# Attention and two feed-forward layers on one core: the four differences of g in the second layer's first product move from VectorE to GpSimd

## The chip, the core and the metric

The kernel runs on one core of one Trainium2 chip. A core has a TensorE (PE in the profile; its weight loads are a row of their own, PEld), a VectorE (DVE), a ScalarE (ACT), a GpSimd (POOL) and a SyncE (SP), which here issues the DMA transfers. Each engine executes its own list of instructions in order, and the engines wait for each other by semaphores. The metric is the device time of the program in microseconds (us); lower is better. The granted TensorE clock is the upper of the two levels (2.4 GHz, shown as 1.00) in all windows below.

## The reference

```python
attn_out = _attn_ref(q, k, v)          # causal attention, window of 64, 4 x 8 heads, 576 x 64
x = attn_out.transpose(0, 2, 1, 3).reshape(2304, 512)
...
r = np.maximum(x @ w_in1, 0.0)         # layer one
x = (r * r) @ w_out1
...
h = x @ w_in2                          # layer two: (2304, 512) @ (512, 2048)
g = np.maximum(0.01 * h, h)
return g @ w_out2                      # (2304, 2048) @ (2048, 512)
```

All arrays are float32. The change lies in the third part, layer two.

## The kernel before

Attention and layer one fill the time up to about 490 us and are not touched. Layer two has two stages, both with a 2 x 2 block scheme of seven products in place of eight: the blocks are called 11, 12, 21 and 22, their sums s1 to s4 on the one side and t1 to t4 on the other. Every product is made with operands that are split in a high and a low part (hi by a cast on ACT, lo = value - hi by a subtraction on DVE, the helpers at L346 and L349) and takes three matmuls: hi hi, hi lo, lo hi.

**First product** (`pair`, L889 to L985). A pair is a choice of one of three pieces of 768 tokens (s) and one of eight pairs of 128 columns of h (p); there are 24. The first six run over p = 0 and 1, then p = 2 to 7 come each with the three pieces. A pair has seven products of six 128x384 matmuls (L889), which collect in four PSUM banks: h, acc, s and t. ACT copies a bank into another as its start (a seed) or into a tile named e, DVE adds (L913) into the pair's tile of g (named m, four blocks of 384), and ACT applies the leaky function (L920) to each block. Then `combine` (L968 to L976) makes four differences for the second stage, in three instructions: the two of tile ta in one (128x768: g1 - g0 and g2 - g1), and the two of tile tb one after the other (128x384: g2 less the first of ta, and g3 less that result). `keep` (L925 to L930) sends g0, the pair g2 and g3, ta and tb to DRAM, as four transfers named gd<-m (twice), gd<-g and gd<-wst. tb lies in the pool "wst" of three tiles, which is also that of the weights wf before they are split; in the last two pairs tb lies in pool "g", which holds ta.

Two things share the engines with the pairs. `x_combos` (L770 to L810) loads a piece of x into a tile m (L773), makes differences in place (L797) and splits them. `w_in` (L841 to L861) loads two blocks of weights into a wst tile (L821, wst<-wf), makes their sums (L835) and splits both. Each is due when the first pair that uses its operands comes near.

**Second product** (`superblock`, L1039 to L1136). For each of the three pieces of tokens seven products of 48 matmuls (L1071) follow. `fetch` (L1025) loads what `keep` stored (w<-gd, m<-gd), `operands` splits it in four units of 128x768, and `w_out` (L995) loads the weights' blocks in two halves (L1001, wst<-wq, 128x1024) and splits those. A product's matmuls go unit by unit, and the tile of a unit is used again by a later product. The first of these products run between the last three pairs.

The order on each engine is not written by hand. Each step is given to a planner with an engine, a cost, a due time, the tiles that it reads and those that it writes; the planner plays the program through with these costs and so gets the order in which the instructions are written for all engines, in which turn the tiles of a pool are given out, and in which order SP issues its transfers. Only the order is kept: on the chip an instruction starts when its engine is free and its semaphores have come. For a step of n elements per partition on DVE the planner reckons `0.15 + n * 0.00106`.

Of the kernel before, what the change touches and what calls it, by code (L numbers as in the profile page):

```python
# [14 lines left out]
ALU = mybir.AluOpType  # L15
# [22 lines left out]
NH = 384  # L38
# [58 lines left out]
class Plan:  # L97
# [38 lines left out]
    def slot(self, pool, tag, shape, dtype=F32, bufs=1):  # L136
        self.bufs.setdefault(tag, bufs)
        return Slot(self, pool, tag, shape, dtype)

    def op(self, engine, cost, due, fn, reads=(), writes=(), needs=(), nbytes=0, margin=0.0, after=()):  # L140

        i = len(self.ops)
        deps = set(after)
        for r in reads:
            if r in self.last_write:
                deps.add(self.last_write[r])
            self.reads_since[r].append(i)
        for w in writes:
            if w in self.last_write:
                deps.add(self.last_write[w])  # L150
            deps.update(self.reads_since.pop(w, ()))
            self.last_write[w] = i
        deps.discard(i)
        slots = {x[0] for x in (*reads, *writes) if isinstance(x[0], Slot)} | set(needs)
        for s in slots:
            s.users += 1
        self.ops.append((engine, cost, due, fn, deps, slots, nbytes, margin))
# [103 lines left out]

def dve_cost(n):
    return 0.15 + n * 0.00106


def dve_fast(n):
# [29 lines left out]
def build(ctx, tc, qp, kp, vp, w1, w2, caps, ident, out, prm=PRM):  # L296
    nc = tc.nc
# [22 lines left out]
    class Late:  # L320

        pool = None
# [12 lines left out]
    op, slot = plan.op, plan.slot  # L335
# [29 lines left out]
    def float_words(s, j, m, c, cv, after=()):  # L365
# [34 lines left out]
        op("act", act_cost(DM), c - prm["AL"], rebias, [(raw, 0)], [(raw, 0)])  # L400
        op("dve", dve_fast(DM), c, conv0, [(raw, 0)], [(cv, 0)])
        op("dve", dve_cost(DM), c + 0.4 * cs, conv1, [(raw, 0)], [(cv, 0)])
        op("dve", dve_cost(DM), c + 1.0 * cs, conv2, [(raw, 0)], [(cv, 0)])

    def weight(k, c, gate=()):

        j, m = divmod(k, 2)
        cv = slot(ep, "e", [P, DM], I32, 4)
        w = slot(rings[f"w{m}"], f"w{m}", [P, 2, DM], F32R)
        wt[j, m] = w  # L410
        cs = prm["CS"]
        float_words(0, j, m, c, cv)
        op("act", act_cost(DM), c + 1.8 * cs, lambda: copy(w.ap[:, 0], f32(cv.ap)), [(cv, 0), *gate], [(w, 0)])
        op(
            "dve", dve_cost(DM), c + 2.5 * cs,
            lambda: sub(nc.vector, w.ap[:, 1], f32(cv.ap), w.ap[:, 0]),
            [(cv, 0), (w, 0)], [(w, 1)],
        )
# [455 lines left out]
    def pair(q, s, p, T, A, last):  # L874
# [93 lines left out]
        def combine(own, k, n, in0, in1, due):  # L968
            views = [(lambda o=o, j=j: o.ap[:, j : j + n]) for o, j in (in0, in1)]
            op(  # L970
                "dve", dve_cost(n * NH), due,
                lambda: nc.vector.tensor_tensor(out=own.ap[:, k : k + n], in0=views[0](), in1=views[1](), op=ALU.subtract),
                [(o, j + h) for o, j in (in0, in1) for h in range(n)], [(own, k + h) for h in range(n)],
            )

        combine(ta, 0, 2, (g, 1), (g, 0), t[8])  # L976
        combine(tb, 0, 1, (g, 2), (ta, 0), t[9])
        combine(tb, 1, 1, (g, 3), (tb, 0), t[9] + 0.6)
        keep(1, lambda: g.ap[:, 2:4], [(g, 2), (g, 3)], t[9])
        keep(3, lambda: ta.ap, [(ta, 0), (ta, 1)], t[9])  # L980
# [210 lines left out]
    if prm["WARM"]:  # L1191
# [3 lines left out]
        for i in range(prm["WARM"]):  # L1195
# [3 lines left out]
                    out=warm_p.ap, lhsT=warm_s.ap, rhs=warm_s.ap, start=True, stop=True  # L1199
# [76 lines left out]
    for q, (p, s) in enumerate(seq):  # L1276
# [4 lines left out]
        if q == len(seq) - 2:  # L1281
            unit_slots()
            plan.pad = 8192
            own = [[slot(rings[t], t, [P, HP, NH]) for t in ("w0", "w1")] for _ in range(2)]
# [68 lines left out]
```

## Time and profile before

| what | value |
|---|---|
| three timed executions, us | 840.36, 841.39, 841.53 |
| their median, us | 841.39 |
| the profiled execution, us | 840.72 |
| its span from the first instruction to the last, us | 838.9 |
| busy share of the span: PE, PEld, DVE, ACT, POOL | 99%, 90%, 67%, 55%, 0% |
| granted TensorE clock | 1.0 |

The span is what the trace covers; 1.8 us of the profiled execution lie outside it. A busy share is the time in which the engine had an instruction in execution, over the whole span. PE's matmuls are pipelined, so that its rows overlap a little and a gap of PE is best read from the row of PEld, which shows when a weight load had to wait and for whom.

### The profile page before, as it was taken

Reading aid. Unit: us, or ns where it says so; the run is one execution under the profiler, and the core shown is the slowest. Engines: PE = TensorE matmul, PEld = TensorE weight load, DVE = VectorE, ACT = ScalarE, POOL = GpSimd, SP = SyncE. Lnnn points to the kernel's source line nnn. Section 1 sums busy time; section 2 is a strip of 40 time slices with the busy share of each in tenths; the row PEclk is TensorE's granted clock in tenths of the full one; section 3 lists DMA queues with packets and bytes.
Section 4 is the critical chain, followed back from the end, with each engine's and each line's share of the span. In section 5 each row is a group of like instructions: output and inputs, shape, how many; then the busy total and the mean of one; then the engine's idle time right before and its main releaser. Section 6 shows DMA issues by size and latency. Waiting matters only on the chain.

```text
span 838.9 us, 14060 instructions
## 1 busy us (share of the span) xinstructions
PE 830.2 (99%) x5344; PEld 751.0 (90%) x5344; DVE 562.7 (67%) x941; ACT 463.7 (55%) x1011; POOL 0.2 (0%) x4
## 2 busy tenths in 40 slices
PE   9999999999999999999999999999999999999998
PEld 8788988888888888888888899999999999999998
DVE  5988687865656666567899657665654887555553
ACT  4978865644354554354444456655565877444441
POOL 0000000000000000000000000000000000000000
PEclk9999999999999999999999999999999999999999
DMA  8665434225434355346874256665557998766661
GB/s 288 220 211 188 146 111 147 83 80 200 144 128 146 129 198 169 127 151 201 298 244 151 73 185 238 223 222 207 209 207 256 373 416 329 247 207 227 206 207 57
DMA packets 77988, 164.64 MB, mean 196 GB/s; under 512 B 6752, under 2 KB 46432, under 8 KB 77920
## 3 DMA queue, kind: packets, MB, share of 16 engines
q1 hardware_dynamic: 77472, 163.21, 56.9%
q8 instruction: 42, 0.69, 0.3%
q10 hardware_dynamic: 448, 0.52, 0.3%
q14 instruction: 26, 0.21, 0.1%
HBM read 108.66 MB, written 55.05 MB: 195 GB/s over the span
## 4 chain that ended last, share of the span: by engine, by line
PE 89%; DMA 5%; DVE 4%; ACT 1%; issue 0%; SPq 0%; ACTq 0%; DVEq 0%
PE h L686 22%; PE acc L698 21%; PE acc L1071 10%; PE h L889 8%; PE s L889 5%; PE h L1071 5%; PE h L698 3%; PE acc L889 3%; PE s L1071 2%; PE t L889 2%; PE t L1071 2%; PE t L552 2%; PE s L479 1%; DMA gd<-g 1%; PE t L543 1%; DMA w<-vp 1%
## 5 line engine op out<-in xcount | busy, mean ns | idle before, releaser
L686 PE MATMUL h<-x,w 128*128 128x512 f32 (+1 forms) x1008 | 214.7, 364 | 1.5 <-DVE x L349 1.3
L686 PEld LDWEIGHTS h<-x,w 128*128 128x128 f32 x1008 | 168.3, 188 | 32.3 <-issue 1.7
L698 PE MATMUL acc<-g,w 128*128 128x512 f32 x576 | 141.5, 392 | 0.0
L698 PEld LDWEIGHTS acc<-g,w 128*128 128x128 f32 x576 | 107.2, 188 | 21.9
L889 PE MATMUL h<-w,x 128*128 128x384 f32 x432 | 83.0, 334 | 0.0
L889 PEld LDWEIGHTS h<-w,x 128*128 128x128 f32 x432 | 75.6, 188 | 0.1
L1071 PE MATMUL acc<-x,w 128*128 128x384 f32 x360 | 73.8, 334 | 0.1
L349 DVE TENSOR_TENSOR x<-m,x 128x768 fp32r<-128x768 f32 x50 | 47.2, 957 | 36.3 <-ACT x L346 36.2
L346 ACT CAST x<-m 128x768 fp32r<-128x768 f32 x50 | 41.2, 837 | 40.9 <-PE h L1071 17.4
L1071 PEld LDWEIGHTS acc<-x,w 128*128 128x128 f32 x360 | 63.4, 188 | 0.4 <-DVE w L349 0.4
L379 ACT ACTIVATE wst<-wst 128x512 f32<-128x512 f32 x64 | 42.7, 673 | 34.0 <-DMA wst<-w1b 14.5
L346 ACT CAST w<-m 128x768 fp32r<-128x768 f32 (+1 forms) x50 | 39.5, 798 | 39.3 <-PE h L1071 10.8
L349 DVE TENSOR_TENSOR w<-m,w 128x768 fp32r<-128x768 f32 (+1 forms) x50 | 44.9, 907 | 20.5 <-ACT w L346 20.3
L657 DVE TENSOR_TENSOR e<-e 128x512 f32<-128x512 f32 x48 | 33.1, 690 | 37.9 <-ACT g L656 37.8
L889 PE MATMUL s<-w,x 128*128 128x384 f32 x288 | 57.8, 335 | 0.0
L652 ACT ACTIVATE e<-h 128x512 f32<-128x512 f32 x48 | 28.5, 594 | 47.2 <-PE h L686 46.1
L889 PEld LDWEIGHTS s<-w,x 128*128 128x128 f32 x288 | 50.5, 188 | 0.4 <-ACT e L346 0.3
L698 PE MATMUL acc<-x,w 128*128 128x512 f32 x192 | 48.1, 394 | 0.0
L388 DVE SCALAR_TENSOR_TENSOR e<-wst,e 128x512 int32<-128x512 int32 x64 | 44.3, 692 | 1.9
L394 DVE SCALAR_TENSOR_TENSOR e<-wst,e 128x512 int32<-128x512 int32 x64 | 44.1, 690 | 1.5
L698 PEld LDWEIGHTS acc<-x,w 128*128 128x128 f32 x192 | 34.6, 189 | 6.3
L511 ACT ACTIVATE u<-u,nm 128x128 f32<-128x128 f32 x64 | 25.0, 392 | 25.4 <-DVE nm L508 25.4
(131 smaller groups left out, 1319.5 us busy)
## 6 DMA issues: line engine op xcount, KB each, us to landing
m<-gd SPq DMA_DIRECT2D x38, 768.0 KB, 4.4
wst<-wq SPq DMA_DIRECT2D x22, 512.0 KB, 7.6
gd<-g SPq DMA_DIRECT2D x26, 384.0 KB, 3.1
gd<-m SPq DMA_DIRECT2D x24, 384.0 KB, 2.7
gd<-wst SPq DMA_DIRECT2D x22, 384.0 KB, 3.2
wst<-w1a SPq DMA_DIRECT2D x16, 512.0 KB, 4.4
v<-vp SPq DMA_DIRECT2D x32, 256.0 KB, 3.3
wst<-w2a SPq DMA_DIRECT2D x16, 512.0 KB, 3.6
```

What stands on the lines that cost most here:

```text
L346: nc.scalar.copy(out=dst, in_=src)
L349: eng.tensor_tensor(out=lo, in0=src, in1=f32(hi), op=ALU.subtract)
L379: nc.scalar.activation(out=top, in_=top, func=AF.Copy, scale=2.0**-112)
L388: nc.vector.scalar_tensor_tensor(out=cv.ap, in0=words(1), scalar=-(1 << 31), in1=cv.ap, op0=ALU.bitwise_and, op1=ALU.bitwise_or,)
L394: nc.vector.scalar_tensor_tensor(out=cv.ap, in0=words(0), scalar=29, in1=cv.ap, op0=ALU.logical_shift_right, op1=ALU.bitwise_or,)
L511: nc.scalar.activation(out=u.ap[:, h, :], in_=u.ap[:, h, :], func=AF.Exp, bias=nm.ap[:, h : h + 1], scale=1.0, accum_out=None if dve_sum e ...
L652: nc.scalar.activation(out=r.ap, in_=hp.ap, func=AF.Relu)
L657: op("dve", dve_cost(n), a0 + 1.4, lambda: nc.vector.tensor_tensor(out=r.ap, in0=r.ap, in1=r.ap, op=ALU.mult), [], [(r, 0)])
L686: nc.tensor.matmul(out=hp.ap, lhsT=wi[:, a, kk, :], rhs=x.ap[:, b, kk, c0 : c0 + n], start=(kk == 0 and m == 0), stop=(kk == KD - 1 and m ...
L698: nc.tensor.matmul(out=a, lhsT=w.ap[:, i, d * P : (d + 1) * P], rhs=g[:, b], start=first and m == 0, stop=last and m == 2, skip_group_chec ...
L889: nc.tensor.matmul(out=ps.ap, lhsT=wc.ap[:, v, k, i * P : (i + 1) * P], rhs=x.ap[:, u, n], start=begin and i == 0 and m == 0, stop=i == 1 ...
L1071: nc.tensor.matmul(out=bank[into][i].ap, lhsT=w.ap[:, v, p, i * P : (i + 1) * P], rhs=u.ap[:, x, e, j], start=begin and n == 0 and j == 0 ...
```

## The change

The three instructions of `combine` in each pair are given to GpSimd, as `nc.gpsimd.tensor_tensor`, and the planner reckons them with a cost of their own. Nothing else of the program text changes. Of the changed kernel all lines behind L266 have numbers that are higher by four.

```diff
@@ -263,6 +263,10 @@
+def pool_cost(n):
+    return 0.2 + n * 0.0021
+
+
 def dve_fast(n):
     return 0.15 + n * 0.00053
...
@@ -968,8 +972,8 @@
         def combine(own, k, n, in0, in1, due):
             views = [(lambda o=o, j=j: o.ap[:, j : j + n]) for o, j in (in0, in1)]
             op(
-                "dve", dve_cost(n * NH), due,
-                lambda: nc.vector.tensor_tensor(out=own.ap[:, k : k + n], in0=views[0](), in1=views[1](), op=ALU.subtract),
+                "pool", pool_cost(n * NH), due,
+                lambda: nc.gpsimd.tensor_tensor(out=own.ap[:, k : k + n], in0=views[0](), in1=views[1](), op=ALU.subtract),
                 [(o, j + h) for o, j in (in0, in1) for h in range(n)], [(own, k + h) for h in range(n)],
             )
```

72 instructions leave DVE's list, 24 of 128x768 and 48 of 128x384, and stand on GpSimd's, which held nothing in the main part of the program. With the other engine and cost the planner comes to another order on all engines. Three places of it matter below.

The first is SP's list while the first pairs run. gd<- are `keep`'s transfers (wst is tb, g is ta, m is g itself), and m<-x_103 are the three loads of a piece of x. Before:

```order
L928 DMA gd<-m 128x2x384
L928 DMA gd<-g 128x2x384
L928 DMA gd<-wst 128x2x384
L773 DMA m<-x_103 128x768
L773 DMA m<-x_103 128x384 x2
```

After:

```order
L932 DMA gd<-m 128x2x384
L932 DMA gd<-g 128x2x384
L777 DMA m<-x_103 128x768
L932 DMA gd<-wst 128x2x384
L777 DMA m<-x_103 128x384 x2
```

The first load of x now stands ahead of the store of tb, the other two behind it as before.

The second is SP's list in the middle of the pairs, about a `w_in`, whose two loads are wst<-wf. The rows run from one pair's last stores to the stores of the next. Before:

```order
L928 DMA gd<-m 128x384
L928 DMA gd<-g 128x2x384
L928 DMA gd<-m 128x2x384
L928 DMA gd<-wst 128x2x384
L821 DMA wst<-wf 128x512 x2
L928 DMA gd<-g 128x2x384
```

After:

```order
L932 DMA gd<-wst 128x2x384
L932 DMA gd<-m 128x384
L825 DMA wst<-wf 128x512 x2
L932 DMA gd<-m 128x2x384
L932 DMA gd<-g 128x2x384
L932 DMA gd<-wst 128x2x384
```

Before, the loads follow the store of tb of a pair; after, the store of g0 of the next pair (gd<-m 128x384) stands between that and the loads.

The third is ACT's list where the pairs give way to the second product. The casts of 128x768 are units of operands fetched from gd, w_6559<-wst is the first half of the weights s1 of the second of these products, and w_6484<-m, after it was renumbered w_6465<-m, is the first unit of an operand used later, whose tile was the third unit's of the first of these products. Before:

```order
L346 CAST x_6518<-w_6321 128x768 x2
L920 ACTIVATE m<-m 128x384 x2
L346 CAST x_6404<-w_6342 128x768 x2
L346 CAST w_6559<-wst 128x1024
L346 COPY e<-acc_306 128x384
L346 COPY e<-acc_276 128x384
L346 CAST w_6484<-m 128x768
```

After:

```order
L350 CAST x_6519<-w_6319 128x768
L924 ACTIVATE m<-m 128x384
L350 CAST x_6519<-w_6319 128x768
L350 CAST w_6465<-m 128x768
L350 CAST w_6559<-wst 128x1024
L350 COPY e<-acc_306 128x384
L350 COPY e<-acc_276 128x384
```

The cast of w<-m has moved from behind the two copies to ahead of the cast of the weights.

## Rows read from the trace of the kernel before

**Rows 1.** Page, part 1: busy us by engine, share of the span, instructions.
```profile
PE 830.2 (99%) x5344; PEld 751.0 (90%) x5344; DVE 562.7 (67%) x941; ACT 463.7 (55%) x1011; POOL 0.2 (0%) x4
```

**Rows 2.** Windows: busy us by engine (and instructions), granted clock, DMA share, GB/s.
```profile
core 0: us, PE busy (x) PEld busy (x) DVE busy (x) ACT busy (x) POOL busy (x), PEclk, DMA share, GB/s
...
497.00:508.00 11.00, 10.66 (x60) 10.03 (x59) 10.83 (x17) 8.21 (x16) 0.00 (x0) 1.00 0.83 286
...
562.00:584.00 22.00, 22.00 (x129) 22.00 (x128) 13.05 (x23) 12.84 (x28) 0.00 (x0) 1.00 0.61 212
...
650.00:676.00 26.00, 25.75 (x147) 25.11 (x146) 21.47 (x27) 19.81 (x32) 0.00 (x0) 1.00 1.03 379
...
760.00:838.90 78.90, 75.50 (x436) 75.18 (x434) 37.12 (x46) 30.34 (x41) 0.00 (x0) 1.00 0.52 174
```

**Rows 3.** Waits of PEld from 470 to 690: us in total, times, longest.
```profile
PEld acc L889 <- ACT acc L346: 1.5, 2, 0.9
PEld t L889 <- ACT m L920: 0.5, 1, 0.5
PEld acc L1071 <- DVE w L349: 0.4, 1, 0.4
PEld s L889 <- ACT e L346: 0.3, 1, 0.3
```

**Rows 4.** Instructions of L972: ns min/median/max, first and last start, form.
```profile
L972 DVE TENSOR_TENSOR g<-m x24: 949/959/960, 497.3 to 665.8; 128x768 f32<-128x768 f32 x24
L972 DVE TENSOR_TENSOR wst<-m,g x22: 557/559/560, 498.3 to 648.1; 128x384 f32<-128x384 f32 x22
```

**Rows 5.** Timeline, first pairs: start, us, engine, line, operation [idle before <-releaser].
```profile
491.27 1.01 PEld L889 LDWEIGHTS acc<-w,x 128*128 128x128 f32 x6 [0.87 <-ACT acc L346]
...
499.97 1.52 SPq L773 DMA_DIRECT2D m<-x  x3
...
502.78 0.84 ACT L346 CAST w<-m 128x768 fp32r<-128x768 f32 x1 [0.81 <-DVE m L797]
...
504.05 1.00 PEld L889 LDWEIGHTS s<-w,x 128*128 128x128 f32 x6 [0.29 <-ACT e L346]
...
506.74 1.01 PEld L889 LDWEIGHTS acc<-w,x 128*128 128x128 f32 x6 [0.65 <-ACT acc L346]
```

**Rows 6.** Timeline, two pairs in the middle, about a w_in.
```profile
570.05 1.96 SPq L821 DMA_DIRECT2D wst<-wf  x2
...
574.72 0.49 ACT L920 ACTIVATE m<-acc 128x384 f32<-128x384 f32 x1
...
577.18 0.62 ACT L346 CAST x<-wst 128x512 fp32r<-128x512 f32 x1
...
580.60 1.05 PEld L889 LDWEIGHTS acc<-w,x 128*128 128x128 f32 x6
```

**Rows 7.** DMA issues from 531.3 to 531.5: KB, median us to landing.
```profile
wst<-wf SPq DMA_DIRECT2D x1, 256.0 KB, 2.8
```

**Rows 8.** DMA issues from 570.0 to 570.1.
```profile
wst<-wf SPq DMA_DIRECT2D x1, 256.0 KB, 4.1
```

**Rows 9.** Timeline, from the last pairs to the second product.
```profile
656.58 1.05 ACT L346 CAST w<-wst 128x1024 fp32r<-128x1024 f32 x1 [1.20 <-DMA wst<-wq]
...
658.07 1.00 PEld L889 LDWEIGHTS t<-w,x 128*128 128x128 f32 x6 [0.50 <-ACT m L920]
...
664.43 4.32 PE L1071 MATMUL acc<-w,w 128*128 128x384 f32 x24
...
666.81 1.05 ACT L346 CAST w<-wst 128x1024 fp32r<-128x1024 f32 x1
...
667.88 1.23 DVE L349 TENSOR_TENSOR w<-wst,w 128x1024 fp32r<-128x1024 f32 x1 [0.24 <-ACT w L346]
...
669.16 0.19 PEld L1071 LDWEIGHTS acc<-x,w 128*128 128x128 f32 x1 [0.39 <-DVE w L349]
669.22 1.57 ACT L346 CAST w<-m 128x768 fp32r<-128x768 f32 x2
```

## The prediction

> **What bounds the kernel now.** I read the page's first part, then windows over the stretch in which the combinations run, then the waits of TensorE there, then the timeline at each of these waits. The page says that PE is busy 99% of the span and VectorE 67% [rows 1]. A share of the span says little about one stage, so the windows come next. In the middle of the pairs PE is busy in all 22.00 us of a window of 22.00 while DVE has 13.05 [rows 2]: there nothing but PE sets the time, and 129 matmuls in 22.00 us make 0.171 us each, 1.02 for a product of six and 7.2 for a pair of 42. In two stretches PE has gaps: among the first pairs, 497 to 508 us, where DVE is busy in 10.83 of 11.00, and where the pairs give way to the second product, 650 to 676, where DVE has 21.47 of 26.00 and the transfers take all there is (DMA share 1.03, 379 GB/s) [rows 2]. Behind 676 no combination runs any more, and the 3.4 us that PE lacks in the last 78.9 are for the end of the program [rows 2].
>
> The waits of PEld from 470 to 690 us say what can be won: 1.5 + 0.5 + 0.4 + 0.3 = 2.7 us [rows 3]. The longest, 0.87 us, falls at 491.27 [rows 5], ahead of the first combination at 497.3 [rows 4]. Four are left: 0.29 at 504.05 and 0.65 at 506.74 [rows 5], 0.50 at 658.07 and 0.39 at 669.16 [rows 9], 1.83 us in all.
>
> **What leaves DVE.** 24 instructions of 0.959 us and 48 of 0.559 (the row shows 22 of these; the others have the same form) [rows 4]: 23.0 + 26.8 = 49.8 us, 9% of DVE's 562.7 [rows 1]. Nearly all of it lies beside a PE that never pauses, and there it is worth 0. It can be worth something only at the four waits, so between 0 and 1.83 us.
>
> **What GpSimd takes for it.** No row shows GpSimd at such work; its four instructions make 0.2 us together [rows 1]. From below, the nearest row is DVE's own time, 0.96 and 0.56, or 2.08 us a pair [rows 4]. From above I take the point from which GpSimd would hold up the pairs, 7.2 us a pair [rows 2], 3.5 times DVE's. Between ends that far apart I take their geometric middle, 1.87 times: 1.8 and 1.05 us, 3.9 a pair. It leaves GpSimd idle for almost half of a pair, so that its own speed costs nothing in the middle pairs; only what waits for it can.
>
> The Trainium skill has a price (GPSIMD Engine Reference, § 3.1): a tensor_tensor of 2048 float32 takes 4497 ns on GpSimd against 2293 on VectorE, 1.96 times. By that a pair would be about 4.1 us, an estimate from that page, and the sum would be the same. No run so far shows it.
>
> **The first pairs.** The cast at 502.78 waited 0.81 us for a DVE difference of x (L797) [rows 5], and the two PE waits behind it are seeds and copies that stand behind such casts on ACT. With 2.08 us a pair gone from DVE that wait may vanish, and PE's 0.29 and 0.65 with it: -0.94. Against it stands the new order on SP. The first load of x now goes out ahead of tb's store and takes a tile of "m" that the combination reads. In DVE's hands the chain of a pair, from 497.3 [rows 4], ends about 497.35 + 0.96 + 2 x 0.56 = 499.4, and the loads go out at 499.97 [rows 5]. In GpSimd's it ends at 497.35 + 1.8 + 2 x 1.05 = 501.25, so the loads go out up to 1.8 us later, and the casts that wait for them stand on ACT ahead of seeds for which PE waits. If all but 0.3 of these 1.8 us reaches PE (the half-full ACT, 8.21 of 11.00 [rows 2], gives a little room), that is +1.5. Between -0.94 and +1.5 I take 0, since one instruction stream loses work exactly where another comes late.
>
> **The middle pairs.** The stores of ta and tb go out some 2 us later; their tiles come round again only pairs later. The loads of a `w_in` are what moves: before, they go out at 570.05, and the cast that uses them starts at 577.18, 7.1 us later [rows 6]. After, they stand on SP behind g0's store of the next pair, which needs the leaky that ends at 574.72 + 0.49 = 575.21 [rows 6], so they go out about 575.7. Landing took 2.8 us in the one place of before where these loads already stand behind that store [rows 7], and 4.1 at 570.05 [rows 8]. They would land at 578.5 or at 579.8. PE wants its seed at 580.60; ahead of it on ACT are the cast, 0.62, and the seed, by the nearest row 0.49 [rows 6]: the loads must be there by 579.5. At 2.8 us there is 1.0 us to spare. I take 2.8, the row of the same pattern, and 0 for this part; the other end is a rival.
>
> **The change of stage.** Two terms. First, m1's and m2's stores of pair 22 now stand ahead of the loads of the weights (wst<-wq), and so these go out later, behind transfers that fill the queues anyway. The cast for which PE's product into t waited indirectly had itself waited 1.20 us for this load [rows 9]. I reckon 0.2 MB more ahead of it, at 379 GB/s [rows 2] 0.5 us: PE's 0.50 at 658.07 becomes 1.0, **+0.5**. Second, ACT's cast of w<-m now stands ahead of the cast of the weights s1. It writes the tile that PE reads until the end of the third unit of the first second-stage product, 664.43 + 4.32 / 2 = 666.6 [rows 9], or 667.1 with the 0.5 from above. The cast takes 1.57 / 2 = 0.79, to 667.9; the weights' cast starts then instead of at 666.81; DVE's lo starts 667.88 - 666.81 = 1.07 later, takes 1.23 and ends at 670.2 instead of 669.11 [rows 9]. So PE's load of 669.16 goes at about 670.25, 1.1 us later, of which 0.5 was there already: **+0.6**. Its range is from 0 (GpSimd's relief lets the cast's neighbours come early and PE's wait stays 0.39) to +3 (the operand that w<-m reads lands only as in before, where the cast starts at 669.22 [rows 9]).
>
> **The sum**, against the profiled execution: 840.72 + 0 (DVE) + 0 (first pairs) + 0 (middle) + 0.5 + 0.6 (change of stage) = 841.8. The profiled execution lies 0.67 us under the median of the three, 841.39, and against that the forecast is 841.39 + 1.1 = **842.5 us**, with 841.2 to 844.0 as its own range. 0.2%, 1.7 us, is about what a measurement of this kernel can tell from no change, so this is "same".
>
> **Rival 1, slower: late weights.** If the loads of a `w_in` land as at 570.05, 4.1 us [rows 8], they come at 579.8 to 580.3 for a deadline of 579.5, and PE stands 0.3 to 0.8 us at each of the five `w_in` that follow this pattern: +1.5 to +4, 844.0 to 846.5. It decides from a landing of 3.8 us on. For it: DMA share 0.61 there [rows 2], and two landings that differ by 1.3 us. Against it: GpSimd's slower chain moves that pair's other stores behind these loads, which leaves them the pattern of rows 7.
>
> **Rival 2, slower: the two engines hinder each other.** Where GpSimd and DVE both read two operands from SBUF, one may have to stand while the other works. GpSimd would then take not 2.08 but 3.9 us of a pair from DVE. In the middle that still fits (13.05 of 22.00 less 3 x 2.08, plus 3 x 3.9, is 18.5 [rows 2, 4]). In the dense stretches it does not: 497 to 508 has 0.17 us free, holds two chains, and would go from 10.83 to 10.83 + 2 x 1.8 = 14.4 in 11; with half of that hidden, as PE has other products ready, +1.7 us: 844.2. No row of before can show it, as GpSimd was idle.
>
> The Trainium skill states this rule (SBUF — State Buffer, § Who interferes with whom): a VectorE instruction with two SBUF inputs contends with a GpSimd instruction that reads SBUF, and the one that comes second waits for the whole of the other. The subtractions of L349 and L797 are of that kind. It is the rule that speaks most against this change.
>
> **Rival 3, faster: DVE's relief removes the four waits.** All 1.83 us go and the loads of x come no later: 841.39 - 1.83 = 839.6. For it: DVE's 10.83 of 11.00. Against it: the load orders above, and that two of the waits are behind transfers [rows 9].
>
> **Rival 4: GpSimd is over 3.5 times slower than DVE** and so becomes the bound of the pairs: at 4 times 8.3 us a pair, 24 x 1.1 = +26 us, 868. Only the missing row speaks for it. That the change would not do what it says is excluded: the 72 instructions stand in GpSimd's list.
>
> **How the numbers follow.** The forecast 0.55, rival 1 0.15, rival 2 0.22, rival 3 0.06, rival 4 0.02. Rival 3 is the part under 839.7. Of the forecast's own range up to 844.0 what lies over 843.1 counts as slower, 0.05. So faster 0.06, same 0.50, slower 0.44. The range: from 840.4, which leaves out rival 3, to 845.6, which leaves out the upper part of rival 1 and rival 4, under 2 in 10 together.
>
> **What would show it.** GpSimd's rows at 1.8 and 1.05 us, done well before the next pair's; DVE at about 513 busy. PEld's waits: two or none at 504 to 507; about 1.0 for the product into t at 658 and again about 1.0 at 669 to 671 with the cast w<-m ahead of the weights' cast on ACT. Rival 1 shows as five waits for a seed into acc, some 22 us apart, each behind a cast that waits for wst<-wf. Rival 2 shows in the durations of L349 and L797 (in the new numbering L353 and L801), stretched where GpSimd is busy. The prediction is wrong if the loads of x, once late, keep the first pairs waiting for more than 1.5 us, or if the order of the second product, which I followed only to its second product's first unit, has moved a wait that I did not look for.

## The result, and the profile after

The changed kernel is slower: 846.04 us against 840.62 (medians of 16 executions each, taken side by side). The ratio over these executions is 1.0072 with a 95% interval of 1.0054 to 1.0090, which is +4.5 to +7.6 us. The forecast was 842.5 with a range up to 845.6.

The two profiled executions differ by only 1.52 us (842.24 against 840.72), and that has to be understood first. Both kernels have executions that lie some 4 us apart. In the two profiled ones this difference arises in the first 17 us, where both run the same list. Timeline of TensorE at the start, before (start, us, engine, line, operation):

```profile
7.92 1.97 PE L479 MATMUL h<-w,w 64*64 64x128 f32 x16
...
27.55 0.53 PEld L686 LDWEIGHTS h<-x,w 128*128 128x128 f32 x4 [0.17 <-ACT w L346]
```

The same of after:

```profile
6.41 1.09 PE L483 MATMUL h<-w,w 64*64 64x128 f32 x16
...
23.56 1.50 PEld L690 LDWEIGHTS h<-x,w 128*128 128x128 f32 x12 [0.17 <-ACT x L350]
```

The same 16 matmuls took 1.97 us in the one and 1.09 in the other, though the windows show a granted clock of 1.00 in both, and layer one began 3.99 us earlier. The profile of after happened to be one with the quick start. So I compare the waits of TensorE, which do not depend on it, and the ratios, which are over many executions of both. Waits of PEld from 470 to 690 us, after (us in total, times, longest):

```profile
PEld h L893 <- ACT e L350: 1.9, 2, 1.0
PEld acc L1075 <- DVE w L353: 1.7, 2, 1.0
PEld s L893 <- ACT e L350: 1.5, 1, 1.5
PEld s L893 <- DVE m L917: 1.4, 2, 0.8
PEld acc L893 <- ACT acc L350: 0.9, 1, 0.9
PEld t L893 <- ACT m L924: 0.6, 1, 0.6
PEld h L893 <- DVE x L353: 0.5, 1, 0.5
PEld acc L1075 <- ACT w L350: 0.2, 1, 0.2
```

They answer to [rows 3]. The 0.9 into acc is the wait that lies ahead of all differences; without it 1.83 us have become 7.68: 5.18 among the first pairs (0.94 before) and 2.50 at the change of stage (0.89 before). The sum grew by 5.85 us. Less the earlier start that is 5.85 - 3.99 = +1.9, against the +1.52 between the two executions; 0.3 lies elsewhere. The ratio puts the loss at 4.5 to 7.6.

The wait of 0.9 into acc also lets the start be left out of the time. It lies at 491.27 before [rows 5], and after at:

```profile
487.24 1.01 PEld L893 LDWEIGHTS acc<-w,x 128*128 128x128 f32 x6 [0.87 <-ACT acc L350]
```

From there to the end of the span it is 838.9 - 491.27 = 347.6 us before and 840.5 - 487.24 = 353.3 after: +5.6, which is about what the waits make.

Page, part 1, and the instructions of `combine` (now L976; ns min/median/max), after:

```profile
PE 826.7 (98%) x5344; PEld 746.2 (89%) x5344; DVE 529.4 (63%) x869; ACT 462.3 (55%) x1011; POOL 102.1 (12%) x76
```

```profile
L976 POOL TENSOR_TENSOR g<-m x24: 1845/1850/2567, 492.7 to 663.4; 128x768 f32<-128x768 f32 x24
L976 POOL TENSOR_TENSOR wst<-m,g x22: 1006/1012/1614, 494.6 to 649.1; 128x384 f32<-128x384 f32 x22
```

GpSimd takes 1.85 and 1.01 us, where 1.8 and 1.05 were reckoned; but the longest took 2.57 and 1.61. And VectorE has not lost the 49.8 us that were taken from it: 562.7 - 49.8 would be 513, and it has 529.4. Some 16.5 us of stretching came in. Where, shows the timeline of after, first pairs:

```profile
492.72 1.85 POOL L976 TENSOR_TENSOR g<-m 128x768 f32<-128x768 f32 x1 [492.28 <-ACT m L924]
492.85 0.56 DVE L917 TENSOR_TENSOR m<-h,e 128x384 f32<-128x384 f32 x1 [0.26 <-PE h L893]
493.40 1.99 DVE L353 TENSOR_TENSOR w<-m,w 128x768 fp32r<-128x768 f32 x1
...
494.65 1.61 POOL L976 TENSOR_TENSOR wst<-m,g 128x384 f32<-128x384 f32 x1
...
497.78 2.27 POOL L976 TENSOR_TENSOR g<-m 128x768 f32<-128x768 f32 x1 [0.24 <-ACT m L924]
...
498.27 2.19 DVE L801 TENSOR_TENSOR m<-m 128x384 f32<-128x384 f32 x1
...
500.50 0.83 ACT L350 CAST w<-m 128x768 fp32r<-128x768 f32 x1 [2.42 <-DVE m L801]
...
501.76 1.00 PEld L893 LDWEIGHTS s<-w,x 128*128 128x128 f32 x6 [1.47 <-ACT e L350]
```

Read it in pairs. L917 at 492.85 has one operand in PSUM (h) and takes its usual 0.56 us in the middle of GpSimd's work. L353 at 493.40 has both operands in SBUF; it takes 1.99 in place of 0.95 and ends 0.82 us behind GpSimd's end (492.72 + 1.85 = 494.57). GpSimd's next, from 494.65, then waits in its turn while L353 still runs, and takes 1.61 for 1.01. At 498.27 a subtraction of 0.56 us takes 2.19 and ends 0.41 behind GpSimd's end of 500.05. The cast on ACT that needs it waits 2.42 us, a seed stands behind the cast, and TensorE waits 1.47. The engine that works second stands still for what is left of the other's instruction.

The same stands at the first `w_in`, after:

```profile
520.62 4.02 DVE L839 TENSOR_TENSOR wst<-wst 128x256 f32<-128x256 f32 x4
...
521.34 1.86 POOL L976 TENSOR_TENSOR g<-m 128x768 f32<-128x768 f32 x1 [3.39 <-ACT m L924]
...
524.68 1.35 ACT L350 CAST x<-wst 128x1024 fp32r<-128x1024 f32 x2 [1.28 <-DVE wst L839]
525.30 0.65 PEld L893 LDWEIGHTS h<-w,x 128*128 128x128 f32 x4 [0.45 <-DVE x L353]
```

Four sums of 0.42 us each take 4.02: the first two keep their time, the third, caught behind this GpSimd instruction, takes 2.08, and the fourth, behind the next one, 1.23. Behind them TensorE waits 0.45, 0.89 and 0.82 us, at 525.30, 526.84 and 528.66, where before it did not wait at all.

In the middle pairs nothing was lost. The timeline about a later `w_in`, after, answers to [rows 6]:

```profile
575.73 0.87 SPq L825 DMA_DIRECT2D wst<-wf  x2
...
579.03 0.60 ACT L350 CAST x<-wst 128x512 fp32r<-128x512 f32 x1
579.54 0.47 ACT L350 COPY acc<-h 128x384 f32<-128x384 f32 x1
...
580.60 1.05 PEld L893 LDWEIGHTS acc<-w,x 128*128 128x128 f32 x6
```

The change of stage, after, answers to [rows 9]:

```profile
658.21 1.00 PEld L893 LDWEIGHTS t<-w,x 128*128 128x128 f32 x6 [0.64 <-ACT m L924]
...
666.89 0.84 ACT L350 CAST w<-m 128x768 fp32r<-128x768 f32 x1 [2.60 <-PE acc L1075]
667.63 1.05 ACT L350 CAST w<-wst 128x1024 fp32r<-128x1024 f32 x1
...
669.99 0.19 PEld L1075 LDWEIGHTS acc<-x,w 128*128 128x128 f32 x1 [0.96 <-DVE w L353]
...
670.64 3.07 POOL L976 TENSOR_TENSOR g<-m,g 128x384 f32<-128x384 f32 x2 [4.71 <-DMA gd<-g]
...
672.76 2.03 DVE L353 TENSOR_TENSOR w<-wst,w 128x1024 fp32r<-128x1024 f32 x1
...
674.85 0.19 PEld L1075 LDWEIGHTS acc<-x,w 128*128 128x128 f32 x1 [0.74 <-DVE w L353]
```

The cast of w<-m stands ahead of the weights' cast and waits for TensorE, as reckoned. The wait at 674.85 was not foreseen: GpSimd stretches a subtraction of 1.22 us to 2.03, and TensorE waits 0.74 for it.

### The profile page after: what moved, and what is told of

Read it like the earlier page. It is cut to its first block, busy times and chain, and to the rows that moved or that the text cites. A ratio compares the mean times of both kernels' runs of the same rounds, so it can differ in the third digit from the quotient of the medians.

```text
span 840.5 us, 14128 instructions
## 1 busy us (share of the span) xinstructions
PE 826.7 (98%) x5344; PEld 746.2 (89%) x5344; DVE 529.4 (63%) x869; ACT 462.3 (55%) x1011; POOL 102.1 (12%) x76
## 4 chain that ended last, share of the span: by engine, by line
PE 89%; DVE 6%; ACT 2%; DMA 2%; issue 1%; SPq 0%; ACTq 0%; DVEq 0%
PE h L690 22%; PE acc L702 21%; PE acc L1075 11%; PE h L893 8%; PE s L893 5%; PE h L1075 5%; PE h L702 3%; PE acc L893 3%; PE t L893 3%; PE s L1075 2%; PE t L1075 2%; PE t L556 2%; PE s L483 2%; PE t L547 1%; DVE w L353 1%; DMA wst<-wq 1%
## 5 line engine op out<-in xcount | busy, mean ns | idle before, releaser
L976 POOL TENSOR_TENSOR g<-m 128x768 f32<-128x768 f32 x24 | 48.6, 2025 | 557.2 <-ACT m L924 557.2
L353 DVE TENSOR_TENSOR x<-m,x 128x768 fp32r<-128x768 f32 x50 | 47.2, 957 | 38.6 <-ACT x L350 38.6
L1075 PEld LDWEIGHTS acc<-x,w 128*128 128x128 f32 x360 | 63.3, 188 | 1.9 <-DVE w L353 1.7
L353 DVE TENSOR_TENSOR w<-m,w 128x768 fp32r<-128x768 f32 (+1 forms) x50 | 48.2, 968 | 24.0 <-ACT w L350 23.7
L917 DVE TENSOR_TENSOR m<-s,e 128x384 f32<-128x384 f32 x24 | 13.3, 556 | 58.5 <-PE s L893 40.5
L924 ACT ACTIVATE m<-m 128x384 f32<-128x384 f32 x51 | 26.8, 526 | 35.0 <-DVE m L917 34.8
L392 DVE SCALAR_TENSOR_TENSOR e<-wst,e 128x512 int32<-128x512 int32 x64 | 44.3, 692 | 1.9
```

What stands on the lines that cost most here:

```text
L353: eng.tensor_tensor(out=lo, in0=src, in1=f32(hi), op=ALU.subtract)
L392: nc.vector.scalar_tensor_tensor(out=cv.ap, in0=words(1), scalar=-(1 << 31), in1=cv.ap, op0=ALU.bitwise_and, op1=ALU.bitwise_or,)
L924: nc.scalar.activation(out=g.ap[:, k], in_=src, func=AF.Prelu, alpha=SLOPE)
L976: lambda: nc.gpsimd.tensor_tensor(out=own.ap[:, k : k + n], in0=views[0](), in1=views[1](), op=ALU.subtract),
L1075: nc.tensor.matmul(out=bank[into][i].ap, lhsT=w.ap[:, v, p, i * P : (i + 1) * P], rhs=u.ap[:, x, e, j], start=begin and n == 0 and j == 0 ...
```

## The experiments

Theory A is rival 2: GpSimd and VectorE exclude each other where both read operands from SBUF. Theory B is the forecast's kind of reason: the new order, above all late loads, costs the time. C is GpSimd's slowness. Two came later: D, that any work of GpSimd holds VectorE up, also work that only writes, and E, that GpSimd holds g longer and so makes the loads of x late. All times are compared with the kernel before on the same chip. "First" is the sum of PEld's waits from the first differences to 530 us, "stage" that from 640 to 677 us, both in the profiled execution.

| run | first | stage | sum | ratio to before, 95% |
|---|---|---|---|---|
| before | 0.94 | 0.89 | 1.83 | 1 |
| changed | 5.18 | 2.50 | 7.68 | 1.0072 (1.0054 to 1.0090) |
| e1_order_only | 1.73 | 1.38 | 3.11 | 1.0008 (0.9985 to 1.0031) |
| e2_engine_only | 2.93 | 2.91 | 5.84 | 1.0066 (1.0039 to 1.0093) |
| e3_middle_pairs | 1.33 | 5.52 | 6.85 | 1.0088 (1.0058 to 1.0117) |
| e4_first_pairs | 5.22 | 1.00 | 6.22 | 1.0042 (1.0014 to 1.0070) |
| e5_write_only | 0 | 1.49 | 1.49 | 0.9998 (0.9973 to 1.0024) |
| e6_middle_old_order | 1.04 | 2.24 | 3.28 | 1.0030 (1.0007 to 1.0053) |
| e7_last_old_order | 1.05 | 1.63 | 2.68 | 1.0025 (1.0005 to 1.0045) |
| e8_later_due | 1.08 | 0.98 | 2.06 | 1.0018 (0.9995 to 1.0040) |
| e9_short_pieces | 2.71 | 1.39 | 4.10 | 1.0025 (0.9999 to 1.0050) |
| e10_short_first | 2.97 | 1.17 | 4.14 | 1.0044 (1.0016 to 1.0071) |
| e11_middle_but_one | 1.06 | 1.69 | 2.75 | 0.9995 (0.9971 to 1.0020) |
| e12_short_old_order | 3.29 | 1.34 | 4.63 | 1.0050 (1.0026 to 1.0075) |
| e13_late_release_only | 1.35 | 1.73 | 3.08 | 1.0003 (0.9977 to 1.0029) |
| e14_reads_only | 0.81 | 2.58 | 3.39 | 1.0047 (1.0025 to 1.0069) |

The stretch from the wait at 487 to 492 us to the end of the span, in which the start has no part, grows over before by what "sum" grows, to 0.2 us, in all runs but three: e3 (+6.8 for +5.0), e9 (+3.9 for +2.3) and e12 (+5.5 for +2.8). In these three the granted clock fell behind a wait (last section). The ratio has the start in it as well: in e14 it is 1.0047, while this stretch grows by 1.6 us, 0.2%.

**Order and engine apart.** The first run keeps the changed kernel's order and gives the work back to VectorE, the second keeps the order of before and gives the work to GpSimd.

```diff
 "pool", pool_cost(n * NH), due,
-lambda: nc.gpsimd.tensor_tensor(
+lambda: nc.vector.tensor_tensor(
```

> The order of the changed kernel on every engine, but the 72 differences are executed by VectorE. Theory A (GpSimd and VectorE exclude each other where both read two operands from SBUF, and so stretch VectorE's subtractions): nothing is stretched, L353 and L801 take 0.95 us for 768 columns as before, and the waits of PEld from the first combination to 677 us sum to 1.8 to 3 instead of 7.7; the time is that of before within 1.5 us. Theory B (the new order on SP, ACT and TensorE, the late loads of x above all, costs the time whoever makes the differences): 5 to 8 us of these waits remain, and the time is that of the changed kernel. Theory C (GpSimd's own slowness, 3.9 us a pair, makes the stores and loads late): as A here.

```diff
-"pool", pool_cost(n * NH), due,
+"dve", dve_cost(n * NH), due,
 lambda: nc.gpsimd.tensor_tensor(
```

> The order of the kernel before on every engine, but the 72 differences are executed by GpSimd. Theory A: L353 and L801 are stretched to 1.3 to 2.6 us wherever GpSimd is busy among the first pairs and from 650 us on; the waits of PEld sum to 5 to 8 us and the time is 4 to 6 us over before. Theory B: the waits sum to about 1.8 us, as before, and the time is that of before. Theory C: the waits come back, 4 us or more, but L353 and L801 keep their 0.95 us.

The order alone makes 3.11 us of waits, 1.3 more than before, and a time that can't be told from it. The engine alone makes 5.84, 4.0 more of the changed kernel's 5.85, and most of the loss in time. B falls as the main cause. The timeline of e2 has the same picture as after, in the old order:

```profile
498.20 2.19 DVE L801 TENSOR_TENSOR m<-m 128x384 f32<-128x384 f32 x1
500.43 0.83 ACT L350 CAST w<-m 128x768 fp32r<-128x768 f32 x1 [2.64 <-DVE m L801]
...
501.69 0.99 PEld L893 LDWEIGHTS s<-w,x 128*128 128x128 f32 x6 [2.04 <-ACT e L350]
```

C, which wanted the subtractions to keep their 0.56 and 0.95, falls with that row.

**The pairs apart.** One run leaves GpSimd the pairs 7 to 20, one the first seven, both planned anew.

```diff
-"pool", pool_cost(n * NH), due,
+"pool" if 6 < q < 21 else "dve", (pool_cost if 6 < q < 21 else dve_cost)(n * NH), due,
-lambda: nc.gpsimd.tensor_tensor(
+lambda: (nc.gpsimd if 6 < q < 21 else nc.vector).tensor_tensor(
```

> GpSimd makes the differences of the pairs 7 to 20 alone, 14 of 24, planned so; VectorE those of the first seven and the last three. Theory A: GpSimd has no dense stretch of VectorE beside it any more; waits of PEld 1.5 to 3 us, time within 1.5 us of before, although some of VectorE's instructions in the middle (L839, L353) are still stretched. Theory B: the order in the middle differs from before as in the changed kernel, so it costs what the middle costs there, nothing, and this run would not tell A from B except at the last pairs. No gain over before: TensorE is busy all the time in the middle.

The second has `q < 7` in these places.

> GpSimd makes the differences of the first seven pairs alone, planned so; VectorE the other 17. Theory A: the waits of PEld before 530 us sum to 4 to 5.5 us, those from 650 to 677 us to about 0.9 as before; time 3 to 5 us over before. If the loss lay in the change of stage, the time would be within 1.5 us of before.

The first seven pairs alone bring back the whole loss of the first pairs, wait for wait: 5.22 us against 5.18. The middle pairs were expected to cost nothing, and cost most of all, though GpSimd does nothing from 650 us on there. The timeline of e3:

```profile
666.37 0.83 ACT L350 CAST w<-m 128x768 fp32r<-128x768 f32 x1 [2.16 <-DMA m<-gd]
...
668.96 0.30 PEld L1075 LDWEIGHTS acc<-x,w 128*128 128x128 f32 x2 [3.19 <-ACT w L350]
```

It is the prediction's second term at the change of stage, beyond its upper end of +3: the cast of w<-m stands ahead of the weights' cast and waits for its load, and TensorE waits 3.19 and 1.74 us for the weights behind it. A new plan drew a bad order there; it says nothing on GpSimd. To see the middle pairs without it, the next run kept the order of before.

**The middle and the end with the order of before.** GpSimd executes the pairs 7 to 20, or only the last three, or 7 to 19.

```diff
 "dve", dve_cost(n * NH), due,
-lambda: nc.vector.tensor_tensor(
+lambda: (nc.gpsimd if 6 < q < 21 else nc.vector).tensor_tensor(
```

> The order of the kernel before on every engine; GpSimd executes the differences of the pairs 7 to 20 alone. The run of the same pairs on GpSimd with an order planned anew lost 5 us of waits between 650 and 677 us, where GpSimd did nothing. If that was the order alone: waits of PEld here 1.8 to 2.5 us, as before, the time within 1 us of before. If GpSimd's work in the middle itself costs (late stores, stretched L839 and L353): waits among the middle pairs or from 650 us on, 3 us or more.

With `q > 20`:

> The order of the kernel before on every engine; GpSimd executes the differences of the last three pairs alone. Theory A: the waits among the first pairs are those of before (0.9), those from 650 to 677 us are 2 to 3.5 us as in the run with the engine alone changed (2.9), since L353 is stretched there; time 1 to 2.5 us over before. If the late leaky and the late stores of the earlier pairs were what made that run wait there: 0.9 as before.

With `6 < q < 20`:

> As the run of the pairs 7 to 20 with the order of before, but pair 20 on VectorE too. There the store of tb of pair 20 went out 1.5 us later, SP's loads of the first operands and of the weights stand behind it, and TensorE's product into t waited 1.43 us instead of 0.50. If that one store is the cause, the wait is 0.3 to 0.6 here and the sum of the waits 1.7 to 2.1; if the middle pairs as a whole are (their stores fill the queues later), it stays at 1.2 or more.

In the middle nothing waits, in any of the three. In e6 the product into t waited 1.43 us instead of 0.50. There the store of tb of pair 20 goes out 4.06 us behind the start of that pair's differences (640.02 - 635.96) against 2.52 before (642.39 - 639.87), and SP's loads stand behind it: a second way in which a slow GpSimd costs time. With pair 20 back on VectorE that wait was 0.91, between what the one store and what the whole middle should give, and the time is that of before. So the store of pair 20 has a part in it; the rest is not settled. The last three pairs alone cost 0.74 us at the change of stage, and TensorE waits 1.21 for L353 instead of 0.39, less than the 2 us at least that I expected.

**Is it the reading?** GpSimd stays busy, but fills in place of reading. All columns but the first of each difference are left out (the edit is shortened here).

```diff
-lambda: nc.gpsimd.tensor_tensor(...)
+tensor_tensor(...) of column 0 alone
+for _ in range(2):
+    nc.gpsimd.memset(own.ap[:, k : k + n, 1:NH], 0.0)
```

> The order of the changed kernel. Each of GpSimd's 72 differences is cut to one column (so that it still waits for g) and followed by two fills with zeros of the other columns of the same tile, which read nothing; the differences themselves are left out. GpSimd is about as busy as in the changed kernel, if a fill takes 0.4 to 1 us, but hardly reads SBUF. Theory A (exclusion where both read SBUF): L353 and L801 keep 0.95 us for 768 columns, up to 0.3 us more where they meet a one-column difference, and the waits of PEld from the first pairs to 677 us sum to 2.5 to 4 us, as with the order alone (3.1), instead of 7.7; the time is 1 to 2 us over before. Theory D (any work of GpSimd in SBUF holds VectorE up, written or read): L353 and L801 are stretched as in the changed kernel and the waits stay at 6 to 8 us.

Instructions of e5 from 490 to 530 us (ns min/median/max):

```profile
L353 DVE TENSOR_TENSOR w<-m,w x8: 559/948/959, 492.8 to 513.1; 128x768 fp32r<-128x768 f32 x6, 128x384 fp32r<-128x384 f32 x2
...
L976 POOL TENSOR_TENSOR g<-m x5: 197/198/953, 497.8 to 523.5; 128x2 f32<-128x2 f32 x5
...
L980 POOL MEMSET g<- x10: 733/739/747, 498.0 to 524.4; 128x766 f32 x10
```

GpSimd is busy 0.20 + 2 x 0.74 us for ta and 0.19 + 2 x 0.42 for each of tb, 3.7 us a pair against 3.9, and L353 is not stretched: at most 959 ns, where in the changed kernel it took up to 2595. Only GpSimd's own short reads, median 198 ns, are held up to 953, the length of one subtraction of VectorE. The waits of the first pairs are gone altogether, those of before too. D falls. This run also gives the most that the change could have won with its order: 1.49 us of waits against 1.83, so 0.3 us.

**Short pieces.** If the exclusion is per instruction, shorter ones should hurt less. e9 has the order of the changed kernel, e10 gives GpSimd the first seven pairs alone, e12 has the order of before (the edit is shortened here).

```diff
-lambda: nc.gpsimd.tensor_tensor(out=own.ap[:, k : k + n], ...)
+for h in range(n):
+    for c in range(0, NH, 128):
+        nc.gpsimd.tensor_tensor(...)   # columns c to c + 128 of block h
```

> The order of the changed kernel; GpSimd makes all the differences, but in pieces of 128 columns, 12 instructions a pair instead of 3, by GpSimd's rows in the changed kernel (1.85 us for 768 columns, 1.01 for 384: 0.17 + 2.19 ns a column) some 0.45 us each, 5.4 us a pair. Theory A in its strict form (the exclusion holds for one instruction, then the other engine has its turn): L353 and L801 wait at most 0.45 us each and take 0.95 to 1.5 us where GpSimd is busy instead of up to 2.6; the waits of PEld from the first pairs to 677 us fall from 7.7 to 3 to 4.5 us, the time is 1 to 2.5 us over before. If the two engines instead share the ports by column, the pieces change nothing: 7 us or more, and GpSimd's longer chain adds to it.

> As the run with GpSimd in the first seven pairs alone, with pieces of 128 columns there. Theory A: the waits before 530 us fall from 5.2 to 1 to 2.5 us, those from 650 us on stay 1.0; time 0 to 1.5 us over before. It beats before only if the waits before 530 us come under 0.8.

> The order of the kernel before, all differences on GpSimd in pieces of 128 columns. Theory A: waits before 530 us fall from 2.9 (whole instructions) to 0.5 to 1.5; from 650 us on the product into t waits as long as with whole instructions or longer, 1.7 to 2.5 us, since tb's store comes later still and SP's loads stand behind it, and the product that waits for L353 0.4 to 0.9 instead of 1.17; sum 3 to 4.5, time 1 to 2.5 us over before.

The stretch fell as A says: in e9 L353 takes at most 1.21 us for 768 columns in the first pairs, and the time comes down from +0.72% to +0.25%. But the waits of the first pairs fell only to 2.71 in e9 and 2.97 in e10 (1 to 2.5 was expected), and in e12 they rose from the 2.93 of e2 to 3.29 (0.5 to 1.5 was expected). At the change of stage e12's product into t waits 0.77, where I expected 1.7 to 2.5. None of the three beats before. The reason stands in the timeline of e9:

```profile
504.22 0.51 ACT L350 CAST w<-m 128x384 fp32r<-128x384 f32 x1 [2.17 <-DMA m<-x]
...
505.16 1.00 PEld L893 LDWEIGHTS h<-w,x 128*128 128x128 f32 x6 [2.34 <-ACT e L350]
```

Now a load of x is late. It overwrites the tile of g of the first pair, and GpSimd reads that tile for longer. Counted from the wait that all runs have at 487 to 492 us (491.27 in before), the load goes out after 8.7 us before, 10.3 in the changed kernel, 9.1 in e5 and 11.4 in e9. So there are two causes among the first pairs, and e5 had taken away both.

**The two causes apart.** The first run holds g as long as the changed kernel but fills instead of reading; the second lets go of g early and then reads tb, its own tile, for 3.0 to 3.6 us among the first pairs. Both leave out all columns of the differences but the first (the edits are shortened here).

```diff
+look()                      # one column of the difference
+memset(...); memset(...)    # as long as the difference takes
+look()
```

> The order of the changed kernel. Each difference is replaced by a one-column difference, fills with zeros that read nothing, and the one-column difference again, so that g is held about as long as in the changed kernel (1.8 us and 1.1 us) but hardly read; the other columns' differences are left out. Theory A alone (the exclusion): waits of PEld before 530 us 0 to 0.6, as with fills alone (0). Theory E (the late release of g and so the late loads of x): the loads of x go out as in the changed kernel, 10.3 us behind the wait at 487 to 492 us that all runs have, and the waits before 530 us are 1.3 to 3.

```diff
+look()                      # for ta, tb 0 and tb 1
+if k == 1:
+    memset(both)
+    tensor_tensor(out=both, in0=both, in1=both) twice
```

> The order of the changed kernel. The three differences of a pair are cut to one column each, so that g is let go early; then GpSimd subtracts the tile of tb from itself twice (768 columns, 1.85 us each, both operands from SBUF), so that it reads two operands about as long as in the changed kernel, 3.7 us a pair, at one stretch and somewhat later. The differences themselves are left out. Theory A: L353, L801 and L839 are stretched up to 2.8 us, and the waits before 530 us are 2.5 to 5. Theory E: the loads of x go out 9 us behind the common wait, and the waits before 530 us are 0 to 0.6.

The late release alone makes 1.35 us, with no subtraction stretched (L353 at most 960 ns): one wait, behind a cast that waits 1.43 for m<-x. The reads alone make 0.81 us there and 0.62 at a place (652 us) where only e6 has one, of 0.15; L353 is stretched to 2.18 and L801 to 1.82, though neither touches the tile that GpSimd reads here, so it is not a shared tile that holds them up. But the reads fall later than in the changed kernel, and L839 at 520 is spared (0.42 each). Nor is e14 free of late loads: the first of x goes out 8.0 us behind the common wait, but the other two stand behind the store of tb and go out 12.6 us behind it, where they went at 11.2 in the changed kernel. I had expected 2.5 to 5. Neither alone gives the 5.18. Of these, the 2.16 us at 525 to 529 have no load of x near them, and e5 and e13, where nothing is stretched, have no wait there: they are the exclusion's. For the 3.02 us at 497 to 504 both are needed, and how they share them stays open.

**An attempt at a better order.** The differences stay on VectorE; those of the first six pairs are due 2 us later.

```diff
+o = 2 if q < 6 else 0.0
-combine(ta, 0, 2, (g, 1), (g, 0), t[8])
+combine(ta, 0, 2, (g, 1), (g, 0), t[8] + o)   # the other two alike
```

> All differences on VectorE, planned with VectorE's cost as before, but those of the first six pairs due 2 us later, so that the splitting of x goes ahead of some of them. If VectorE's queue is what makes TensorE wait at 504 and 507 us, the 0.94 us there shrink, to 0 at best, and the time falls by up to 1 us; the order also changes on SP and ACT, and may take 0.5 to 1.5 us for that, as the order of the changed kernel did when VectorE executed it (1.7 instead of 0.9).

One wait of 1.08 us took the place of the two of 0.94. No gain.

## Why the prediction was wrong

**What held.** TensorE bounds the kernel, and the middle pairs cost nothing: the loads of a `w_in` went out at 575.73, where 575.7 was reckoned, landed in 3.2 us, where 2.8 was taken and 3.8 was the limit, and the seed was there when TensorE came. That the times agree as they stand is luck: the earlier start and the new waits nearly cancel there, so that TensorE's load stands at 580.60 in both profiles. GpSimd's durations, 1.8 and 1.05 us, were right to 4%; they were the geometric middle of two far ends, so that is luck as well. The order at the change of stage cost what it was said to cost, nearly: the product into t waits 0.64 in place of 0.50 (+0.14 for +0.5 reckoned), and the load behind the weights s1 0.96 + 0.16 in place of 0.39 (+0.73 for +0.6): +0.87 for +1.1. The second is the order's: e1, with VectorE at the work, has the same 0.96 + 0.16. Rival 1 did not come, rival 4 did not, and rival 3's gain is bounded by e5 at 0.3 us of the 1.83.

**The step that failed** is the term of the first pairs: "Between -0.94 and +1.5 I take 0, since one instruction stream loses work exactly where another comes late." It measured 5.18 - 0.94 = +4.24. VectorE's stream did not lose the work. The late loads were seen rightly (10.3 against 8.7, 1.6 us late, for up to 1.8), and alone they cost 1.35 us (e13, against none in e5), within that range. What was missing was rival 2, which stood in the text with 0.22.

**Rival 2 had the mechanism and a price that was too low.** It reckoned +1.7 for 497 to 508 us; there the waits grew by 3.02 - 0.94 = 2.1. But it stopped at 508, since "in the middle that still fits", by the busy time of a whole window. From 508 to 530 us VectorE was busy in 13.8 of 22 us, room enough by that count, and TensorE waited 2.16 us at 525 to 529 all the same, for a chain: four sums in a row, the last two caught behind a GpSimd instruction each, a cast and a seed behind them. And the last 0.74 us, at 674.85, are of the same kind. Together 4.24 + 0.87 + 0.74 = 5.85.

The Trainium skill (SBUF — State Buffer, § Who interferes with whom) states the rule, and every run here agrees with it: a subtraction with two SBUF inputs is held up by a GpSimd instruction that reads SBUF (2.19 us for 0.56), not by one that only writes (0.95 throughout in e5), and one with an input in PSUM is not (0.56 at 492.85, and at most 0.56 in every addition of L917 in the changed kernel). I gave it too small a chance for want of a row; the traces of before could not show it.

## What to carry to other kernels

An elementwise operation with two SBUF operands that is moved from VectorE to GpSimd does not wholly leave VectorE; here a third of the 49.8 us came back as stretching. Where VectorE works on two SBUF operands as well, count GpSimd's longer time as VectorE's, as the upper end, and ask chain by chain, not by a window's busy share, who waits for an instruction that may take two to five times as long. It is harmless where nothing waits for VectorE (here the middle pairs), and shorter instructions on GpSimd shorten the stretch (e9), though here they did not pay. Then look for what the slower engine holds longer: the tile that a load wants next, and the queue behind its store.

## What the runs showed that I had not expected

- GpSimd's subtraction costs about 0.17 us and 2.19 ns a column (1.85 us for 768, 1.01 for 384), a fill under 1 ns a column (0.74 us for 766); a subtraction whose operands are both the tile that it writes took 1.47 us for 766 columns.
- After some long waits TensorE ran slower for a while. In e3, behind its wait of 3.19 us, the granted clock was the lower level of 1.2 GHz for a short stretch:

```profile
670.00:672.00 2.00, 1.01 (x3) 1.01 (x4) 2.00 (x3) 1.83 (x2) 0.00 (x0) 0.68 1.02 397
672.00:674.00 2.00, 2.00 (x7) 2.00 (x7) 2.00 (x2) 0.09 (x1) 0.00 (x0) 0.50 1.15 383
674.00:676.00 2.00, 2.00 (x12) 2.00 (x12) 0.42 (x2) 0.84 (x1) 0.00 (x0) 0.96 0.87 321
```

The columns are those of [rows 2]. From 490 to 530 us the clock was 0.96 in e9 (a wait of 2.34) and 0.91 in e12 (3.29), but 1.00 in e10 (2.60). So a wait can cost more than its length: e3, e9 and e12 are the runs whose time grew by 1.6 to 2.7 us more than their waits.
- The start of the program, which no change here touches, moves the time by some 4 us from one execution to the next, more than most of these effects: the common wait lies between 487.2 and 492.4 us in the sixteen profiles. Waits in the trace, and many executions, had to stand in for a single pair of times.
